# An attention and FFN kernel on one core: one segment's transposes moved from TensorE to DMA, the last output tile in column halves, and a new order of the instructions

## The chip, the core and the metric

The kernel runs on one core of a Trainium2 chip. A core has five engines that work in parallel, each through its own instructions in order: TensorE (PE, matrix products), VectorE (DVE), ScalarE (ACT), GpSimd (POOL) and SyncE (SP, which here only issues DMAs). The metric is the time of one execution on the device in microseconds (us); lower is better.

## The reference

Two identical layers work on x of 2048 tokens by 512 features in bf16. Each layer is an attention with a compressive memory (32 heads of 16, four segments of 512 tokens) and then a gated FFN of width 1376, each on a layer-normalised input and added back to x:

```python
def _A_ref(x, wq, wk, wv, wo, beta):        # x: layer-normalised
    q, k, v = ...                           # x @ wq, x @ wk, x @ wv, by heads and segments
    for s in range(4):
        p = softmax(qs @ ks.T * scale + causal_mask)
        a_dot = p @ vs
        pq = phi(qs)                        # phi(t) = t + 1 if t > 0 else exp(t)
        a_mem = (pq @ M) / (pq @ z + 1e-6)
        o = g * a_mem + (1 - g) * a_dot     # g = sigmoid(beta), one a head
        M = M + phi(ks).T @ vs
        z = z + phi(ks).sum(over tokens)
    return concat(o) @ wo

def _B_ref(x, w1, w3, w2):                  # x: layer-normalised
    return (silu(x @ w1) * (x @ w3)) @ w2

for layer in range(2):
    x = x + _A_ref(_layernorm(x), ...)
    x = x + _B_ref(_layernorm(x), ...)
```

## The kernel before

The kernel's x stays in on-chip memory as 16 tiles of 128 tokens (`x_tok`); a segment is four tiles. Both layers run through the four segments, so there are eight steps, g = 0 to 7 (g = 4 * layer + segment). Every step does the following.

- **Layer norm** (`layer_norm`): statistics of each tile on DVE (`bnst` L604, `bnag` L606), variance plus epsilon (`lnve` L609), the power -1/2 on POOL (`lnrs` L611), and the normalised tile `xn` (`norm`, L618; two tiles share an xn buffer). The products need x with the features on the partitions, so each tile is then transposed. With `turn` set, TensorE does that in four 128x128 transposes a tile into PSUM (`xt`, L628), and an engine copies the result out (`evt`). Otherwise one DMA transpose on SP's queue turns two tiles at once (`xT`, L634). Before the change `turn` holds for the attention's layer norm of g = 0 and g = 1; all other layer norms go by DMA.
- **Projections** (`project`): q and k by groups of heads (L677), v by tiles (L672), each four products that add up in a PSUM bank, then a copy out on ACT or DVE.
- **Attention** (`attention`): units of logits, four row groups of TensorE side by side (L852), one exponential on ACT for each (L861), the causal mask of the diagonal blocks on POOL (L874), and the weighted values (`attend`, L903). Their results go by a DMA transpose on SP (`XT`, L913) to the division on DVE and POOL (`normalise`, L928 to L941) and by another one (`oT`, L944) to the output projection (L952).
- **Memory** (`phi`, `memory_update`, `memory_read`): phi of k is transposed by DMA (`pkT`, L725) and contracted with v on TensorE (`dacc`, L738); phi of q reads the memory.
- **FFN** (`ffn`): gate and up products (L983), tanh on ACT (L994), two DVE operations (L996, L1000), down products (L1011), and the sum into `x_tok` (`resB`, L1016). In the last layer each tile is then stored (`stx`, issued on SP at L470).

The order on every engine comes from a list scheduler (`Sched.schedule`) that runs when the kernel is built. Each operation has an estimated duration and latency, a priority, and gates (operations that must have been placed before it). The tables `SLACK`, `LOOK`, `MARGIN`, `PRIO`, `GATE` and the constant `C_AGE` steer its choices: `PRIO` shifts the priority of the operations of one name in one step, `GATE` moves the attention unit behind which they may come, `MARGIN` makes an operation's inputs count as later, and `C_AGE` is how long a weighted-values product waits for a moment at which TensorE is not in the midst of full-size products. `dmaT` gives the scheduler its estimate for a DMA transpose. Once chosen, the order is fixed: each engine executes its list in order and waits on semaphores where an input is not ready.

The weights of the FFN and the later x tiles are loaded while step 0 runs (on SP and POOL queues). TensorE's work of later steps fills the gaps between the units of attention of earlier ones: the projections of step 1 run between the logits of step 0, the FFN of step 0 between those of step 1, and so on. After the last attention unit (in the second half of step 7) only the FFN is left.

Of the kernel before, what the change touches and what calls it, by code (L numbers as in the profile page):

```python
# [4 lines left out]
ALU = mybir.AluOpType  # L5
# [3 lines left out]
P = 128  # L9
T = 2048  # L10
# [19 lines left out]
PE_SWITCH = 100.0  # L30
PE_TAIL = 170.0
R_SLACK = 0.0
SLACK = {"pe": 30.0, "act": 60.0, "dve": 60.0, "pool": 0.0, "sp": 30.0}
LOOK = {"pe": 90.0, "act": 10.0, "dve": 10.0, "pool": 5.0, "sp": 200.0}
C_AGE = 1200.0
MARGIN = {"XT": 800.0, "bnst": 50.0, "dacc": 300.0, "evv": 200.0, "g": 100.0, "km": 2000.0, "macc": 100.0, "mde": 1200.0, "mnum": 500.0, "mrec": 200.0, "norm": 50.0, "o": 50.0, "oT": 2000.0, "rd": 200.0, "rdg": 100.0, "resB": 500.0, "stx": 3000.0, "v": 100.0, "xT": 2000.0, "xt": 500.0}


class Pool:
# [328 lines left out]
def o_pe(ns):  # L368
# [4 lines left out]


PRIO = {
    ("bnag", 1): 500.3, ("bnag", 2): 4, ("bnag", 3): 500.15, ("bnag", 4): 300, ("evX", 0): 285.6, ("evk", 1): 700,
    ("evk", 6): -299.6, ("g", 3): -0.05, ("g", 6): -5, ("gp", 0): 19.85, ("hm", 3): 1050, ("hm", 5): -50.05,
    ("k", 3): -0.6, ("k", 4): -2, ("k", 5): 21.4, ("k", 7): 0.15, ("lnve", 5): 500, ("mblk", 2): 300,
    ("mnum", 6): -950.6, ("oT", 3): -600, ("ph", 7): -20, ("phmin", 1): 0.3, ("q", 1): -300, ("q", 6): -1248.55,
    ("q", 7): 0.05, ("rd", 5): -800, ("rdg", 1): 300, ("rdg", 7): -1000, ("resA", 4): -300, ("t", 3): -1000,  # L380
    ("t", 7): -900.4, ("u", 4): -1000, ("v", 1): 2, ("v", 6): -50,
}
GATE = {
    ("bnst", 2): -4, ("bnst", 3): 2, ("bnst", 4): -1, ("km", 7): 14, ("ph", 0): -21, ("phexp", 0): -10, ("v", 0): 2,
    ("v", 1): -45, ("v", 5): -13, ("v", 6): 6, ("v", 7): 8,
}


def build(nc, A_x, A_wq, A_wk, A_wv, A_wo, A_beta, B_w1, B_w3, B_w2, out):
# [6 lines left out]
    def new(name):  # L396
        return Buf(pools[name])
# [67 lines left out]
    def pe(fn, ns, mode="F", **k):  # L465
        return S.add([o_pe(ns)], fn, mode=mode, **k)
# [2 lines left out]
        occ = 60.0 if q != "pool" else 1000.0  # L469
        return S.add([(q, occ, 2000.0)], lambda e: e.dma_start(out_ap, in_ap), dmaq=q, size=size, prio=prio, **k)  # L470

    def dmaT(fn, q="sp", **k):
        return S.add([(q, 1290.0, 2500.0) if k.pop("narrow", False) else (q, 1400.0, 3000.0)], fn, dmaq=q, mode="T", **k)

    def ev(dst, src, n, **k):

# [119 lines left out]
    def layer_norm(s, name, prio, gates=(), fine=False, turn=False, part=(0, LT), dst=None):  # L596
# [17 lines left out]
        for i in tiles:  # L614
# [7 lines left out]
            if turn:  # L622
                B = new("B")
                tb = lambda B=B: bank(B).bitcast(BF16)[:, 0:512].rearrange("p (g c) -> p g c", g=NCG)

                def flip(e, xn=xn, k=k, tb=tb):
                    for cg in range(NCG):
                        o = e.transpose(tb()[:, cg, :], xn_r[xn.slot][:, k, 128 * cg:128 * cg + 128], ident[:])  # L628
                    return o
                pe(flip, 4 * 62, reads=[(xn, k), "ident"], writes=[(B, 0)], bufs=[B, xn], prio=-900, name="xt")  # L630
                ev(lambda i=i: dt_[dst.slot][:, i, :].rearrange("p (g c) -> p g c", c=P), tb, 512, reads=[(B, 0)], writes=[(dst, i)],
                   bufs=[B, dst], prio=-900, name="evt")
            elif k == 1:
                dmaT(lambda e, i=i, xn=xn: e.dma_start_transpose(  # L634
                    dt_[dst.slot][:, i - 1:i + 1, :].rearrange("p i (g c) -> p (i g) c", c=P), xn_r[xn.slot][:].rearrange("p i d -> p (i d)")),
                     reads=[(xn, 0), (xn, 1)], writes=[(dst, i - 1), (dst, i)], bufs=[xn, dst], prio=prio, name="xT")
        return dst


# [82 lines left out]
    def memory_update(g, z, pkb):  # L722
        kt = new("W")
        for hf in range(2):
            dmaT(lambda e, hf=hf: e.dma_start_transpose(  # L725
                pkt_r[kt.slot][:, 2 * hf:2 * hf + 2, :, :].rearrange("p g i c -> p (g i) c"),
                pk_r[pkb.slot][:, 2 * hf:2 * hf + 2, :].rearrange("p g n -> p (g n)")),
                 reads=[(pkb, hf)], writes=[(kt, hf)], bufs=[pkb, kt], prio=g + 0.1, name="pkT")
        mb = new("mb")
        for hf in range(2):  # L730
            B = new("B")
# [155 lines left out]
    def attend(s, g, z, pr, part, G, ees, where, xg, gates):  # L887
# [22 lines left out]
        for a, X in enumerate(Xs):  # L910
            ev(lambda a=a: xs_r[xs.slot][:, a, :], lambda X=X: bank(X), 512, reads=[(X, 0)], writes=[(xs, a)], bufs=[X, xs],
               prio=g - 100.2, name="evX")
        dmaT(lambda e: e.dma_start_transpose(xg_r[xg.slot][:, 0:n, :], xs_r[xs.slot][:].rearrange("p a n -> p (a n)")[:, 0:128 * n]),  # L913
             reads=[(xs, a) for a in range(len(Xs))], writes=[(xg, 0)], bufs=[xs, xg], prio=pr, name="XT", narrow=n == 4)

    def normalise(g, z, part, G, xg, oms):

# [22 lines left out]
        if oms is not None:  # L940
# [2 lines left out]
                writes=[(og, 0), (og, 1)], bufs=[og, oms[G]], prio=pr, name="oadd")  # L943
        dmaT(lambda e: e.dma_start_transpose(  # L944
            ot_r[z.ot.slot][:, G, 128 * t0:128 * t1].rearrange("p (t c) -> p t c", t=nt), fl(og_r, og)),
             reads=[(og, 0), (og, 1)], writes=[(z.ot, G, t) for t in range(t0, t1)], bufs=[og, z.ot], prio=pr, name="oT", narrow=True)

    def out_proj(s, g, z, part):
        for i in range(*part):
# [10 lines left out]
    def ffn(s, g, X, part, last=False):  # L960
# [43 lines left out]
        for i in range(t0, t1):  # L1004
            B = new("B")
            tt = 4 * s + i
            for ft in range(NFT):
                fw = width(ft)
                h, c = of[ft]
# [8 lines left out]
            if last:  # L1018
                ov = out[0].rearrange("(t p) d -> p t d", p=P)
                dma("sp", ov[:, tt, :], x_tok[:, tt, :], 131072, prio=base, reads=[("x", tt)], name="stx")  # L1020


    for layer in range(2):
        for s in range(NS):
# [1 line left out]
            S.cur = g  # L1026
            n0 = len(S.ops)
            X = layer_norm(s, "xa", g - 1.0, gates=[(0, 2) if g == 1 else (0, 13) if g == 2 else (g - 2, 13)],
                           fine=(g == 0), turn=g <= 1)
            if g == 0:  # L1030
                done = [op for op in S.ops[n0:] if op.name == "bnst"][-1:]
                second_loads(LOADS + ("" if LATE_AT is not None else LATE), dict(gates=done, after=done))
# [66 lines left out]
```

The softmax here doesn't subtract the row's maximum and nothing guards it: scores larger than these inputs give would overflow.

## Time and profile before

| | |
|---|---|
| median of 6 runs | 496.1 us (493.36 to 502.42) |
| the profiled execution | 493.74 us |
| its span, first to last instruction | 492.0 us |
| mean granted TensorE clock in it | 0.995 |
| PE busy | 477.1 us, 97% |
| DVE busy | 401.2 us, 82% |
| ACT busy | 390.7 us, 79% |
| POOL busy | 251.6 us, 51% |

Durations in the text come from the profiled execution. A row of the timeline gives start and length in us, the engine, the line of the kernel, the operation, what it writes and reads, and how many instructions were merged; the bracket at its end gives the idle time of the engine before it and what ended that. In the table by stage each engine's busy time in the stage stands with its number of instructions, then the granted clock, the share of the DMA engines and the GB/s they moved. In the list of waits, the total, the number and the longest wait follow the pair that waited and was waited for. Matmuls overlap, so the length of one matmul holds both its streaming time and its latency: the distance of the starts in a row of equal ones is what it costs.

### The profile page before, as it was taken

Reading aid. Unit: us, or ns where it says so; the run is one execution under the profiler, and the core shown is the slowest. Engines: PE = TensorE matmul, PEld = TensorE weight load, DVE = VectorE, ACT = ScalarE, POOL = GpSimd, SP = SyncE. Lnnn points to the kernel's source line nnn. Section 1 sums busy time; section 2 is a strip of 40 time slices with the busy share of each in tenths; the row PEclk is TensorE's granted clock in tenths of the full one; section 3 lists DMA queues with packets and bytes.
Section 4 is the critical chain, followed back from the end, with each engine's and each line's share of the span. In section 5 each row is a group of like instructions: output and inputs, shape, how many; then the busy total and the mean of one; then the engine's idle time right before and its main releaser. Section 6 shows DMA issues by size and latency. Waiting matters only on the chain.

```text
span 492.0 us, 10341 instructions
## 1 busy us (share of the span) xinstructions
PE 477.1 (97%) x4155; PEld 216.6 (44%) x4198; DVE 401.2 (82%) x803; ACT 390.7 (79%) x344; POOL 251.6 (51%) x379
## 2 busy tenths in 40 slices
PE   8989999999999999999999999899999999999997
PEld 4434346754444444334443444444444434444443
DVE  5899999997998888889976899688984687478672
ACT  3979998988988987899888999689987989830230
POOL 4847555765565546556554447565564546520000
PEclk9989999999999999999999999999999999999999
DMA  8665843331233334432442515521153215210301
GB/s 281 222 103 129 150 81 71 77 68 41 55 75 71 64 54 57 61 65 55 66 87 23 86 24 103 69 55 34 32 87 75 46 23 76 76 32 15 82 1 43
DMA packets 101983, 35.84 MB, mean 73 GB/s; under 512 B 94800, under 2 KB 99920, under 8 KB 101936
## 3 DMA queue, kind: packets, MB, share of 16 engines
q1 hardware_dynamic: 99488, 30.36, 30.2%
q0 software_dynamic: 1488, 4.03, 4.1%
q10 hardware_dynamic: 960, 0.79, 0.5%
q8 instruction: 33, 0.54, 0.5%
q14 instruction: 14, 0.11, 0.1%
HBM read 8.43 MB, written 2.10 MB: 21 GB/s over the span
## 4 chain that ended last, share of the span: by engine, by line
PE 79%; DVE 10%; ACT 8%; DMA 2%; issue 1%; POOL 0%; DVEq 0%
PE psall L983 29%; PE psall L1011 15%; PE psall L852 9%; PE psall L677 8%; PE psall L903 6%; ACT e L861 6%; PE psall L952 4%; PE psall L672 4%; DMA W<-W 1%; DVE ln L604 1%; ACT px L712 1%; DVE W L480 1%; DVE xn L618 1%; PE psall L738 1%; DVE x_tok L956 1%
## 5 line engine op out<-in xcount | busy, mean ns | idle before, releaser
L861 ACT ACTIVATE e<-psall 128x2048 bf16<-128x2048 f32 (+1 forms) x180 | 301.5, 1710 | 39.6 <-PE psall L852 37.4
L874 POOL TENSOR_SCALAR_AFFINE_SELECT e<-e 128x512 bf16<-128x512 bf16 x256 | 164.2, 661 | 157.9 <-ACT e L861 157.2
L983 PE MATMUL psall<-W,w 128*128 128x512 bf16 (+2 forms) x792 | 172.6, 357 | 0.4 <-DVE gp L996 0.2
L983 PEld LDWEIGHTS psall<-W,w 128*128 128x128 bf16 (+1 forms) x792 | 73.7, 100 | 74.5 <-issue 12.4
L1011 PE MATMUL psall<-w,h 128*128 128x512 bf16 (+1 forms) x332 | 82.1, 380 | 1.4 <-issue 0.8
L994 ACT ACTIVATE th<-psall 128x512 bf16<-128x512 f32 (+1 forms) x89 | 51.1, 593 | 35.0 <-PE psall L983 34.9
L996 DVE SCALAR_TENSOR_TENSOR gp<-th,psall 128x512 bf16<-128x512 bf16 (+1 forms) x89 | 58.7, 673 | 19.6 <-ACT th L994 18.9
L1000 DVE SCALAR_TENSOR_TENSOR h<-gp,psall 128x512 bf16<-128x512 bf16 (+1 forms) x89 | 59.7, 672 | 8.7 <-PE psall L983 8.1
L1011 PEld LDWEIGHTS psall<-w,h 128*128 128x128 bf16 (+1 forms) x352 | 32.5, 98 | 38.2 <-issue 5.6
L604 DVE BATCH_NORM_STATS2 ln<-x_tok 128x6 f32<-128x512 bf16 x64 | 42.8, 684 | 1.2 <-DMA x_tok<-in_A_x_dram 0.6
L852 PE MATMUL psall<-W 16*128 16x256 bf16 (+3 forms) x544 | 41.8, 295 | 1.4 <-ACT e L861 0.8
L1016 DVE TENSOR_TENSOR x_tok<-psall,x_tok 128x512 bf16<-128x512 f32 x32 | 22.0, 688 | 25.8 <-PE psall L1011 25.7
L852 PE MATMUL psall<-W,km 32*128 32x256 bf16 (+3 forms) x544 | 41.3, 292 | 0.6 <-ACT e L861 0.6
L903 PE MATMUL psall<-e,va 128*32 128x256 bf16 (+3 forms) x1088 | 41.2, 293 | 0.6 <-DVE x_tok L1016 0.2
L480 DVE CAST W<-psall 128x512 bf16<-128x512 f32 x51 | 34.1, 680 | 5.0 <-PE psall L677 4.8
L936 POOL TENSOR_TENSOR og<-xg,rd 128x256 bf16<-128x256 bf16 (+1 forms) x40 | 26.9, 679 | 20.6 <-DVE rd L930 16.4
L677 PE MATMUL psall<-W,wk 128*128 128x512 bf16 (+1 forms) x144 | 35.4, 357 | 0.9 <-ACT W L479 0.9
L480 DVE CAST xs<-psall 128x512 bf16<-128x512 f32 x40 | 26.8, 683 | 10.2 <-PE psall L903 10.1
L618 DVE TENSOR_SCALAR xn<-x_tok,ln 128x512 bf16<-128x512 bf16 x64 | 32.8, 546 | 2.8 <-POOL ln L611 2.8
L672 PE MATMUL psall<-wv,W 128*128 128x512 bf16 x116 | 32.8, 391 | 1.0 <-issue 0.3
L677 PE MATMUL psall<-W,wq 128*128 128x512 bf16 (+1 forms) x144 | 33.1, 357 | 0.3 <-issue 0.3
L852 PEld LDWEIGHTS psall<-W 16*128 16x128 bf16 x544 | 13.2, 91 | 44.6 <-ACT e L861 38.5
(65 smaller groups left out, 447.6 us busy)
## 6 DMA issues: line engine op xcount, KB each, us to landing
w<-in_B_w_dram SPq DMA_DIRECT2D x4, 688.0 KB, 8.2
out_dram<-x_tok SPq DMA_DIRECT2D x16, 128.0 KB, 1.7
km<-W POOLq DMA_DIRECT2D x24, 64.0 KB, 2.9
w<-in_B_w_dram POOLq DMA_DIRECT2D x3, 384.0 KB, 3.9
x_tok<-in_A_x_dram POOLq DMA_DIRECT2D x2, 512.0 KB, 5.0
xg<-xs SPq DMA_TRANSPOSE x36, 2.8
W<-og SPq DMA_TRANSPOSE x36, 2.4
wk<-in_A_wk_dram SPq DMA_DIRECT2D x1, 512.0 KB, 4.2
```

What stands on the lines that cost most here:

```text
L480: return e.tensor_copy(dst(), src())
L672: fn = lambda e, cg=cg, G=G, B=B, st=st, sp_=sp_: e.matmul(bank(B), xa_r[X.slot][:, G, 128 * cg:128 * cg + 128], wv_sb[:, cg, :], start=st ...
L677: fn = lambda e, cg=cg, G=G, B=B, st=st, sp_=sp_, w=w, a=a, W=W, c0=c0: e.matmul(bank(B)[:, W * a:W * a + W], w[:, cg, 128 * G:128 * G + 1 ...
L852: o = e.matmul(S4[:, sps(pg), c:c + n], kk[32 * pg:32 * pg + r, G, 128 * j:128 * j + 128], q_r[z.q.slot][32 * pg:32 * pg + r, G, 128 * t1 ...
L861: act(lambda e, N=N, ebuf=ebuf, pgs=pgs, sps=sps: e.activation(e_r[ebuf.slot][:, pgs[0]:pgs[-1] + 1, 0:N], S4[:, sps(pgs[0]):sps(pgs[-1]) ...
L874: pool(lambda e, ebuf=ebuf, c=c: e.affine_select(e_r[ebuf.slot][:, :, c:c + 128], e_r[ebuf.slot][:, :, c:c + 128], pattern=[[0, 4], [1, 128]],
L903: o = e.matmul(bank(X)[32 * pg:32 * pg + 32, base + W - n:base + W], va_r[z.va.slot][:, j, h:h + 32], e_r[eb.slot][:, pg, c:c + n], start= ...
L983: prev = pe(lambda e, i=i, cg=cg, ft=ft, B=B, w=w: e.matmul(bank(B)[0:width(ft), W * i:W * i + W], w[:, cg, 128 * ft:128 * ft + width(ft)] ...
L994: act(lambda e, fw=fw, NW=NW, B=B, th=th: e.activation(th_r[th.slot][0:fw, 0:NW], bank(B)[0:fw, 0:NW], ACT.Tanh, scale=0.5), NW, reads=[(B ...
L996: dve(lambda e, fw=fw, NW=NW, B=B, th=th, gp=gp: e.scalar_tensor_tensor(gp_r[gp.slot][0:fw, 0:NW], th_r[th.slot][0:fw, 0:NW], 1.0, bank(B) ...
L1000: dve(lambda e, fw=fw, NW=NW, B=B, gp=gps[fg], h=hs[fg]: e.scalar_tensor_tensor(h_r[h.slot][0:fw, 0:NW], gp_r[gp.slot][0:fw, 0:NW], 0.5, b ...
L1011: prev = pe(lambda e, ft=ft, fw=fw, B=B, h=h, c=c: e.matmul(bank(B), h_r[h.slot][0:fw, c:c + 128], w2_sb[0:fw, ft, :], start=(ft == 0), st ...
```

## The change

Four edits. (1) The attention's layer norm of step g = 1 goes by two DMA transposes of two tiles each in place of sixteen TensorE transposes and four copies. (2) The very last output tile is computed in two halves of 256 columns, each with its own sum and its own store. (3) The scheduler's estimate of a DMA transpose's occupancy is 1250 ns for all, and its latency is given by kind. (4) The steering tables have new values, so the order of the instructions on every engine is a new one.

```diff
-SLACK = {"pe": 30.0, "act": 60.0, "dve": 60.0, "pool": 0.0, "sp": 30.0}
-LOOK = {"pe": 90.0, "act": 10.0, "dve": 10.0, "pool": 5.0, "sp": 200.0}
-C_AGE = 1200.0
-MARGIN = {"XT": 800.0, "bnst": 50.0, ...}
+SLACK = {"pe": 30.0, "act": 30.0, "dve": 60.0, "pool": 60.0, "sp": 60.0}
+LOOK = {"pe": 90.0, "act": 60.0, "dve": 5.0, "pool": 60.0, "sp": 10.0}
+C_AGE = 4000.0
+MARGIN = {"bnag": 500.0, "bnst": 300.0, ...}
...
 PRIO = {
...
+    ("bnag", 3): 0.05, ("bnag", 4): 301, ("bnag", 7): 0.3, ("bnst", 1): -500, ("bnst", 5): 500.15, ("d", 3): -500,
...
 GATE = {
-    ("bnst", 2): -4, ("bnst", 3): 2, ("bnst", 4): -1, ("km", 7): 14, ("ph", 0): -21, ("phexp", 0): -10, ("v", 0): 2,
-    ("v", 1): -45, ("v", 5): -13, ("v", 6): 6, ("v", 7): 8,
+    ("bnst", 2): -17, ("bnst", 3): 1, ("ph", 0): -22, ("phexp", 0): -6, ("v", 0): 2, ("v", 1): -59, ("v", 3): 2,
+    ("v", 7): 8,
 }
...
-    def dmaT(fn, q="sp", **k):
-        return S.add([(q, 1290.0, 2500.0) if k.pop("narrow", False) else (q, 1400.0, 3000.0)], fn, dmaq=q, mode="T", **k)
+    def dmaT(fn, lat, q="sp", **k):
+        return S.add([(q, 1250.0, lat)], fn, dmaq=q, mode="T", **k)
...
+            if last and i == LT - 1 and ENDS > 1:
+                n = finish(s, g, tt, t0, of, base, step, n, prev)
+                continue
...
+    ENDS = 2
+
+    def finish(s, g, tt, t0, of, base, step, n, prev):
+
+        ov = out[0].rearrange("(t p) d -> p t d", p=P)
+        for c0 in range(0, D, D // ENDS):
+            cs, B = slice(c0, c0 + D // ENDS), new("B")
+            for ft in range(NFT):
...
+                prev = pe(lambda e, ft=ft, fw=fw, B=B, h=h, c=c, cs=cs: e.matmul(
+                    bank(B)[:, 0:D // ENDS], h_r[h.slot][0:fw, c:c + 128], w2_sb[0:fw, ft, cs], start=(ft == 0), stop=(ft == NFT - 1)),
...
+            dve(lambda e, B=B, cs=cs: e.tensor_tensor(x_tok[:, tt, cs], bank(B)[:, 0:D // ENDS], x_tok[:, tt, cs], ALU.add), D // ENDS, True,
...
+            dma("sp", ov[:, tt, cs], x_tok[:, tt, cs], 131072 // ENDS, prio=base, reads=[("x", tt, c0)], name="stx")
...
-                           fine=(g == 0), turn=g <= 1)
+                           fine=(g == 0), turn=g <= 0)
```

The latencies given by kind are 3300 ns for xT and pkT (3000 before), 2400 for oT and the narrow XT (2500 before) and 2800 for the wide XT (3000 before).

## The prediction

> **What bounds the kernel now.** I read the page's engine table first, then the waits of TensorE, then tables by stage, and then the timeline of the one stage that stood out.
>
> ```profile
> PE 477.1 (97%) x4155; PEld 216.6 (44%) x4198; DVE 401.2 (82%) x803; ACT 390.7 (79%) x344; POOL 251.6 (51%) x379
> PEclk9989999999999999999999999999999999999999
> ```
>
> TensorE (PE) is busy nearly all the time and no other engine is near it. So a microsecond in which PE stands still, or does work it need not do, is a microsecond of the total: after segment 0 there is always projection or FFN work queued on it. The second row has one lower digit, the third slice (24.6 to 36.9 us). The table by stage, 24 to 42 us in steps of 6, and the waits of PE and of ScalarE (ACT) there:
>
> ```profile
> core 0: us, PE busy (x) PEld busy (x) DVE busy (x) ACT busy (x) POOL busy (x), PEclk, DMA share, GB/s
> 24.00:30.00 6.00, 4.55 (x68) 2.04 (x68) 5.42 (x8) 6.00 (x7) 5.01 (x8) 0.99 1.15 146
> 30.00:36.00 6.00, 5.84 (x40) 2.16 (x37) 5.11 (x13) 3.51 (x4) 0.48 (x1) 0.72 0.38 77
> 36.00:42.00 6.00, 6.00 (x92) 3.10 (x89) 5.62 (x18) 6.00 (x9) 2.89 (x6) 1.00 0.25 68
> ...
> PE psall L628 <- DVE xn L618: 1.3, 1, 1.3
> ...
> ACT e L861 <- PE psall L852: 2.5, 2, 2.2
> ```
>
> PE idles, then runs at a granted clock of 0.72, and ACT, full before and after, has 2.5 us without logits. The timeline names the cause:
>
> ```profile
> 26.27 2.89 DVE L618 TENSOR_SCALAR xn<-x_tok,ln 128x512 bf16<-128x512 bf16 x1
> ...
> 27.67 0.27 PE L852 MATMUL psall<-W,km 32*128 32x256 bf16 x2
> 29.22 0.40 PE L628 MATMUL psall<-ident,xn 128*128 128x128 bf16 x4 [1.28 <-DVE xn L618]
> ...
> 31.02 0.63 PE L628 MATMUL psall<-ident,xn 128*128 128x128 bf16 x4
> ```
>
> L628 is segment 1's TensorE transpose. It stands in PE's in-order stream behind a normalisation (L618) that took 2.89 us where its neighbours take 0.40; everything behind it, the logits for ACT included, waits. So the path around 27 to 34 us is this transpose, not ACT.
>
> **The change, part by part.** All against the profiled execution, 493.74 us with a span of 492.0; the median of the runs shown is 496.1, 2.4 more, and I carry the difference over.
>
> *Transposes off PE.* The 1.28 us wait at 29.22 goes, because no PE instruction reads xn of segment 1 any more. The slow clock cost (1 - 0.99) x 6 + (1 - 0.72) x 6 = 1.74 us. Sixteen transposes go: a group of four lasts 0.40 and one alone 0.219, so they start (0.40 - 0.219) / 3 = 0.06 apart and cost 16 x 0.06 = 0.97. Some ran in the slow stretch and are counted twice there, 0.2 off. Sum: 1.28 + 1.74 + 0.97 - 0.2 = 3.8 us. The four 0.40 us copies of their results leave VectorE (DVE), 1.6 us of a 93% busy stretch; that only speeds the casts that PE waits for now and then, and I book nothing for it.
>
> [...]
>
> *Transposes onto the DMA queue.* Two more issues on SP, 1.3 us each there. The same shape (W<-xn, 28 of them) lands 3.0 to 5.7 us after issue:
>
> ```profile
> L634 SPq DMA_TRANSPOSE W<-xn x28: 1231/1306/3075, 52.9 to 456.7; - x28
> ...
> DMA to landing us min/median/max: 3.0/3.2/5.7
> ```
>
> In today's order the last normalisation ends at 31.02 + 0.39 = 31.4, so x would land at 34.6 to 37.1; today the last copy ends at about 38.0 (37.58 + 0.42). So x is not later, but it comes in two lumps, and PE has less to fill with in between: today segment 1's V products run between 32 and 38. Without filler PE has 0.32 us of logits per exponential of 5.61 / 6 = 0.94, thus 0.62 idle of each 0.94. Four microseconds of that would be 2.6, less two memory contractions of 0.55. Bounds 0 to 2.6; the new order raises segment 1's statistics (bnst, 500 earlier; they start at 16.2 now though their load went out at 5.96), so I take the low side, +0.7. On SP the two issues wait for L618, and behind them in line stand XT and pkT, which go out between 24 and 33 us; those feed the division of segment 0's outputs and the memory contraction. SP issues nothing from 33.4 to 40.96, so a wait of some microseconds there is taken up again, and I book none.
>
> [...]
>
> *The last tile by halves.* The end of the timeline:
>
> ```profile
> 488.76 0.69 DVE L1016 TENSOR_TENSOR x_tok<-psall,x_tok 128x512 bf16<-128x512 f32 x1 [1.69 <-PE psall L1011]
> 489.48 0.33 SPq L470 DMA_DIRECT2D out_dram<-x_tok  x1
> ```
>
> 22 matmuls of 256 columns (L677 at 8.66 us: 8 last 1.05, one 0.27, so 0.11 apart) replace 11 of 512 (43 in 9.46: 0.216 apart): 2.44 against 2.37, +0.07. The last add is half as wide: 0.41 for a 256-column DVE operation from PSUM in this profile (L996's 96x256 form), against 0.69, -0.28. Then a 64 KB store in place of 128 KB (1.7 us to landing): between 0 and -0.3, I take -0.1, as the fixed part of 1.7 us should dominate. Nothing hides this, it is the end of the chain. Sum -0.3; bounds -0.5 and +0.1.
>
> *The new order and latencies.* All other queues may be reordered. From 60 to 480 us PE's listed waits that are real (a DMA, ACT, DVE) come to 1.0 for the contraction at L738, 0.6 for ACT and about 1.2 in pieces of 0.2: at most -2.8 to gain. To lose there is more: one late transpose costs about what L738's wait did, 1.0, and a new order may hold several; I bound it at +4. Value 0, as neither sign has a row for it.
>
> Sum: -3.8 + 0.7 - 0.3 + 0 = -3.4: 490.3 for a profiled execution, 492.7 beside the median of 496.1. Own range: stall term from 0 to 2.6, so -4.1 to -1.5, 492.0 to 494.6.
>
> **The rivals.** *The wait only moves (same).* The normalisation at 26.27 is what was late; if it stays late and slow (GpSimd's masks run at 25.44 to 29.0 beside it), PE will wait at segment 1's first projection instead. For it: DVE is over 90% busy there. Against: PE can go on with logits meanwhile, so ACT stays fed. Only the transposes and the end are won: -0.97 - 0.3 = -1.3, 494.8.
>
> *Segment 1's x comes too late (slower).* SP issues in order. If an xT is placed behind the XT that goes out at 40.96, it lands at about 42.2 + 3.2, the second at 46 to 47. PE has run out of filler at about 33.5; each later microsecond costs 0.62 / 0.94 = 0.66. Break-even is where this eats 3.8 + 0.3 = 4.1 us, x at 39.7; slower by 2.5 us takes 6.6 / 0.66 = 10 us, x at 43.5. With x at 45, the first landing, the idle time is 7.6, +3.5: 499.6. For it: early landings are the slow ones (median 4.0 us for the XT before 60 us, 2.8 over the run), since the weights share the DMA engines. Against: SP is idle in between, and nothing forces that place.
>
> *More is won.* The order also closes the other waits: -3.4 - 2.8 = -6.2, 489.9. For it are only the 2.8 us themselves.
>
> That the change does not do what it says has little room: the 16 transposes are gone from PE by a flag.
>
> **How the numbers follow.** Forecast 0.46, wait moves 0.22, x too late 0.22, more won 0.10. About 0.5% (2.5 us) is what a measurement of this kernel can tell from no change. The last third of the forecast's range lies within it; as its likely values crowd at the other end I give that 0.06. Faster: 0.40 + 0.10 = 0.50; same: 0.22 + 0.06 = 0.28; slower: 0.22. The range runs from 489.5 (-6.6, just past the best case) to 500.0 (+3.9, half of the late case beyond it): 0.11 + 0.04 are left out. It holds cases of both signs; the likeliest one's range is 492.0 to 494.6.
>
> **What would show it.** Right: 16 records of the transpose line in place of 32, no PE wait for xn behind 20 us, granted clock 1.00 from 30 to 36 us, ACT's 2.2 us wait gone, 30 W<-xn transposes with two before 40 us landing in 3 to 6 us, 17 output stores, the last add near 0.41 us. Wrong: the slow clock is still there or has moved; PE waits at segment 1's projections for a DMA; new PE waits over 1 us behind 60 us, which would make the order, not the transposes, the main term.

## The result and the profile after

The change made the kernel slower. The ratio of its time to the time before, on the same chip, is 1.0065, with a 95% interval of 1.0049 to 1.0081. The median is 498.52 us (495.29 to 502.41, 32 runs) beside 494.74 us for the kernel before (67 runs, which take the place of the six of the table). So 0.0065 x 494.74 = 3.2 us were lost, where a gain of 3.4 was forecast (the two medians lie 3.8 us apart; the ratio, from runs on the same chip, is the better measure). The profiled execution of the changed kernel took 497.77 us, with a span of 496.0 and a mean granted clock of 0.990 (before 0.995).

The page's engine table and its row of the TensorE clock, after:

```profile
PE 478.5 (96%) x4185; PEld 220.0 (44%) x4226; DVE 394.7 (80%) x796; ACT 393.6 (79%) x350; POOL 250.3 (50%) x380
PEclk9987999999999999999999999999999999999999
```

PE executes 4185 matmuls in place of 4155 (16 transposes fewer, 44 products more from the halves of four tiles; a trace can miss a few records) and is as busy as before. The clock row has two low digits where there was one. The table by stage of the changed kernel, 24 to 48 us:

```profile
core 0: us, PE busy (x) PEld busy (x) DVE busy (x) ACT busy (x) POOL busy (x), PEclk, DMA share, GB/s
24.00:30.00 6.00, 5.62 (x76) 2.28 (x76) 5.31 (x8) 6.00 (x8) 5.43 (x9) 1.00 1.03 159
30.00:36.00 6.00, 3.13 (x25) 1.33 (x26) 6.00 (x17) 3.83 (x5) 0.46 (x1) 0.70 1.08 171
36.00:42.00 6.00, 6.00 (x57) 2.45 (x56) 2.82 (x12) 4.13 (x6) 2.63 (x4) 0.50 0.15 36
42.00:48.00 6.00, 6.00 (x81) 2.40 (x80) 5.35 (x14) 5.50 (x7) 4.70 (x8) 0.95 0.53 136
```

This is the main reading. Between 30 and 36 us PE is busy for 3.13 of 6 us, in 25 matmuls (before: 5.84, in 40). Between 36 and 42 it is busy all the time, but at half clock: 57 matmuls in place of 92. ACT, full there before, has 4.13. The clock costs (0.30 + 0.50 + 0.05) x 6 = 5.1 us of PE time, where the stages from 24 to 36 us cost 1.74 before. The slow stretch has not gone; it is three times as dear.

What PE waited for between 20 and 100 us (total, number, longest), and its timeline from 29 us:

```profile
PE psall L737 <- DVE va L479: 1.9, 1, 1.9
PE psall L851 <- ACT e L860: 1.5, 2, 0.8
PE psall L902 <- POOL e L873: 0.9, 1, 0.9
PE psall L982 <- DVE om L781: 0.6, 1, 0.6
```

```profile
29.18 0.60 PE L671 MATMUL psall<-wv,W 128*128 128x512 bf16 x2
30.50 0.28 PE L851 MATMUL psall<-W 16*128 16x256 bf16 x2 [0.71 <-ACT e L860]
30.62 0.27 PE L851 MATMUL psall<-W,km 32*128 32x256 bf16 x2
32.78 1.09 PE L737 MATMUL psall<-va,W 128*128 128x136 bf16 x8 [1.89 <-DVE va L479]
33.80 0.40 PE L851 MATMUL psall<-W 16*128 16x256 bf16 x4
...
34.76 0.63 PE L671 MATMUL psall<-wv,W 128*128 128x512 bf16 x1 [0.33 <-issue]
```

After the last V products of segment 0 at 29.2 us PE has four small logits products (16 and 32 rows) and then waits 1.89 us for a copy of V (`va`) before the first memory contraction. Segment 1's first full product starts only at 34.76 (two products of that form last 0.60 us at 29.18 and, at half clock, 1.03 at 36.07). The same time on DVE, on GpSimd (POOL) and on SP's queue:

```profile
26.88 2.72 DVE L617 TENSOR_SCALAR xn<-x_tok,ln 128x512 bf16<-128x512 bf16 x1
...
29.78 0.72 DVE L617 TENSOR_SCALAR xn<-x_tok,ln 128x512 bf16<-128x512 bf16 x2
...
32.10 0.62 DVE L479 CAST va<-psall 128x512 bf16<-128x512 f32 x1
```

```profile
25.89 3.56 POOL L873 TENSOR_SCALAR_AFFINE_SELECT e<-e 128x512 bf16<-128x512 bf16 x6
```

```profile
30.21 2.61 SPq L633 DMA_TRANSPOSE W<-xn  x2
```

The first normalisation of segment 1 is again late and long (2.72 us, as 2.89 before) beside six of GpSimd's masks, and holds up the copies of V behind it on DVE. The two transposes go out from 30.21 on and land 3.3 and 3.1 us after their issue, so x comes in two lumps, at 33.5 and 34.7 us.

Where the time is lost can be followed on one milestone per step. The first exponential of step 1 starts at 59.27 us after, 56.85 before: 2.42 later, of which 0.44 are there from the start. The last exponential of the kernel starts at 432.40, before at 428.62: 3.78 later. So some 2 of the 3.3 us that arise between start and last exponential arise before 60 us. The other part shows from 60 to 120 us (before, then after, same columns as in the table by stage):

```profile
60.00:120.00 60.00, 58.78 (x625) 33.63 (x621) 55.34 (x116) 54.48 (x46) 35.09 (x54) 1.00 0.35 71
```

```profile
60.00:120.00 60.00, 56.72 (x627) 32.41 (x631) 53.78 (x111) 53.47 (x46) 35.17 (x55) 1.00 0.44 71
```

PE is busy for 2.06 us less at full clock, in new waits at 61, 67 and 87 us.

The end, the two last sums on DVE:

```profile
491.51 0.42 DVE L1040 TENSOR_TENSOR x_tok<-psall,x_tok 128x256 bf16<-128x256 f32 x1 [0.51 <-PE psall L1035]
492.71 0.42 DVE L1040 TENSOR_TENSOR x_tok<-psall,x_tok 128x256 bf16<-128x256 f32 x1 [0.78 <-PE psall L1035]
```

From the start of the last product to the landing of the last store it is 2.30 us, before 2.83: 0.53 won. But SP then goes through its closing semaphore waits one by one, most of them 0.06 us after the one before (in the trace of after one takes 0.37), and the span ends 1.32 us behind that landing, before 0.83. From last product to end the two kernels differ by 0.04 us (3.62 and 3.66).

**One number for a run.** A profile is one execution; the granted clock and the span are known for every one. Clock lost = (1 - mean granted clock) x span. The kernel before has a slow state, which 15 of its executions in the experiments show, with 12 to 16 us lost, and which this comparison leaves out. Before, the median over the other 91 runs is 1.5 us (10th to 90th percentile 0 to 3.5); after, it is 8.4 over 32 runs (3.6 to 11.9). A line through the runs gives a span of 491.2 + 0.94 x lost before and 491.6 + 0.62 x lost after (correlations 0.83 and 0.94). At no lost clock the two kernels would be within 0.4 us of each other. The profiled execution of after, with 5.0 lost, is one of its milder ones. The traces list the clock itself: it is 1.00 or 0.50 and nothing between. Before, it is 0.50 for 3.41 us from 29.9 us on; after, for 10.24 us from 32.4 on (each trace has one more such stretch, which begins at about the program's end). Clock lost goes through the experiments; it adds up all slow stretches of a run, wherever they lie.

### The profile page after: what moved, and what is told of

Read it like the earlier page. It is cut to its first block, busy times and chain, and to the rows that moved or that the text cites. A ratio compares the mean times of both kernels' runs of the same rounds, so it can differ in the third digit from the quotient of the medians.

```text
span 496.0 us, 10405 instructions
## 1 busy us (share of the span) xinstructions
PE 478.5 (96%) x4185; PEld 220.0 (44%) x4226; DVE 394.7 (80%) x796; ACT 393.6 (79%) x350; POOL 250.3 (50%) x380
## 4 chain that ended last, share of the span: by engine, by line
PE 76%; DVE 11%; ACT 7%; DMA 3%; issue 2%; POOL 0%; ACTq 0%; DVEq 0%
PE psall L982 28%; PE psall L1013 14%; PE psall L851 9%; PE psall L676 8%; PE psall L902 7%; ACT e L860 5%; PE psall L951 4%; PE psall L671 3%; PE psall L1035 2%; DMA xg<-xs 2%; DVE xn L617 1%; DVE W L715 1%; PE psall L737 1%; DVE va L479 1%; DVE gp L995 1%
## 5 line engine op out<-in xcount | busy, mean ns | idle before, releaser
L982 PE MATMUL psall<-W,w 128*128 128x512 bf16 (+3 forms) x792 | 171.1, 356 | 1.3 <-DVE om L781 0.6
L993 ACT ACTIVATE th<-psall 128x512 bf16<-128x512 f32 (+2 forms) x89 | 51.4, 594 | 35.9 <-PE psall L982 35.3
L995 DVE SCALAR_TENSOR_TENSOR gp<-th,psall 128x512 bf16<-128x512 bf16 (+2 forms) x89 | 58.9, 672 | 19.3 <-ACT th L993 18.7
L1013 PE MATMUL psall<-w,h 128*128 128x512 bf16 (+1 forms) x291 | 71.6, 380 | 1.3 <-issue 0.5
L1013 PEld LDWEIGHTS psall<-w,h 128*128 128x128 bf16 (+1 forms) x308 | 28.2, 98 | 34.7 <-issue 5.2
L479 DVE CAST W<-psall 128x512 bf16<-128x512 f32 x46 | 31.1, 681 | 8.2 <-PE psall L676 7.8
L1018 DVE TENSOR_TENSOR x_tok<-psall,x_tok 128x512 bf16<-128x512 f32 x28 | 19.3, 688 | 21.2 <-PE psall L1013 21.2
L676 PE MATMUL psall<-W,wq 128*128 128x512 bf16 (+1 forms) x144 | 35.2, 360 | 0.0
L902 PEld LDWEIGHTS psall<-e,va 128*32 128x32 bf16 x1088 | 24.3, 97 | 20.1 <-issue 3.2
```

Source lines behind the costliest of these rows:

```text
L479: return e.tensor_copy(dst(), src())
L676: fn = lambda e, cg=cg, G=G, B=B, st=st, sp_=sp_, w=w, a=a, W=W, c0=c0: e.matmul(bank(B)[:, W * a:W * a + W], w[:, cg, 128 * G:128 * G + 1 ...
L902: o = e.matmul(bank(X)[32 * pg:32 * pg + 32, base + W - n:base + W], va_r[z.va.slot][:, j, h:h + 32], e_r[eb.slot][:, pg, c:c + n], start= ...
L982: prev = pe(lambda e, i=i, cg=cg, ft=ft, B=B, w=w: e.matmul(bank(B)[0:width(ft), W * i:W * i + W], w[:, cg, 128 * ft:128 * ft + width(ft)] ...
L993: act(lambda e, fw=fw, NW=NW, B=B, th=th: e.activation(th_r[th.slot][0:fw, 0:NW], bank(B)[0:fw, 0:NW], ACT.Tanh, scale=0.5), NW, reads=[(B ...
L995: dve(lambda e, fw=fw, NW=NW, B=B, th=th, gp=gp: e.scalar_tensor_tensor(gp_r[gp.slot][0:fw, 0:NW], th_r[th.slot][0:fw, 0:NW], 1.0, bank(B) ...
```

## The experiments

Theory A: PE has too little to do between 30 and 34 us because segment 1's x comes in two lumps by DMA, its clock falls to half and stays there, and that is the loss. Rivals: the 1.89 us wait for `va` is the root and any order without it is fast; the half clock is only a sign and the new order loses the time elsewhere; the tail or the DMA queues lose it.

All edits but one (interleaved normalisation) leave the scheduler alone. They change its finished order: `move(a, b)` puts operation a behind b on its engine, `fill(n, b, d)` puts n idle 512-column products on TensorE behind b, into the PSUM bank that d is to use and before d, and `find` picks an operation by engine, name and step. All else keeps its place. Ratios are to the kernel before on the same chip; medians taken on different chips are compared less closely than ratios.

**The wait for `va` taken away.** The memory contraction goes behind segment 1's last V product.

```diff
 # the changed kernel
+self.move(self.find("pe", "dacc", 0), self.find("pe", "v0.3", 1))
```

> The changed kernel with one instruction group moved: segment 0's first memory contraction goes behind segment 1's first four V products on TensorE. Theory A (the loss is made early: TensorE stands 2.05 us in front of this contraction at 30.6 us, and the half clock of 10.2 us follows from that idle stretch): the wait for the cast of va goes, ACT's 2.2 us wait for logits at 34.4 shrinks, the slow clock falls to one window of 3.4 us or none, total 2 to 5 us below the changed kernel, ratio to the kernel before 0.997 to 1.002. Rival B (the loss comes from the new order behind 60 us): the total stays within 1 us of the changed kernel, ratio 1.005 or more.

Measured: 496.43 us, 1.0066 [1.0043, 1.0089], as after. Clock lost 5.7. PE's waits between 20 and 100 us:

```profile
PE psall L904 <- ACT e L913: 2.5, 4, 0.8
...
PE psall L724 <- DMA W<-xn: 0.9, 1, 0.9
```

The wait for `va` is gone, and four waits for ACT and one for x itself stand in its place. The ratio is the rival's (1.005 or more), but not for the rival's reason: the slow stretch is still there, 6.83 us from 33.6 us on. So the wait for `va` was not the root: PE had nothing to do, whatever it waited for.

**Idle products as filler.** Three before the small logits at 30.5 us and eight before the contraction, all of full size (128 rows).

```diff
 # the changed kernel; d = self.find("pe", "dacc", 0)
+self.fill(3, self.find("pe", "v3.3", 0), d)
+self.fill(8, self.find("pe", "R1.3", 0), d)
```

> The changed kernel with 11 idle 512-column products added on TensorE, 3 in front of the logits at 30.5 us and 8 in front of the contraction that waits; nothing else is moved and their results are overwritten. Theory A with the clock as the carrier: the waits stay, but the granted clock stays at 1.00 between 30 and 43 us, and the total falls by about half of the slow 10.2 us, 3 to 5 us, ratio 0.997 to 1.001. Rival (the slow clock is not owed to the idle stretch, or the waits alone make the loss): granted clock as in the changed kernel, the total the same or up to 2.4 us longer, ratio 1.005 to 1.012.

Measured: 495.23 us, 1.0024 [1.0006, 1.0043], clock lost 1.5. By stage, 30 to 42 us:

```profile
30.00:36.00 6.00, 5.30 (x41) 1.88 (x41) 6.00 (x16) 4.44 (x6) 0.98 (x2) 1.00 0.80 154
36.00:42.00 6.00, 6.00 (x85) 2.68 (x86) 5.49 (x20) 6.00 (x8) 4.60 (x7) 1.00 0.35 91
```

Eleven products whose results nobody reads make the kernel 0.4% faster. The clock is 1.00, PE does 85 matmuls from 36 to 42 in place of 57 (none of them idle ones, which end at 32.8), and ACT is full again. But PE, now earlier, waits 2.7 us, from 55.7 to 58.4 us, for a transpose of the attention's output (`oT`, W<-og), and the one slow stretch that is left in this trace, 3.41 us, begins at 58.3. That wait is the second loss.

**The tail alone.** The halves put into the kernel before (the function `finish` and its call, nothing else).

```diff
 # the kernel before
+if last and i == LT - 1 and ENDS > 1:
+    n = finish(s, g, tt, t0, of, base, step, n, prev)
+    continue
```

> The kernel before with the column halves alone (the flag holds for the last tile of each of the last layer's four segments). Theory: the last store lands 0.5 us sooner behind the last product, but SP's closing waits run one after another and give it back, so the span behind the last product stays at 3.6 us and the total within 0.5 us of the kernel before, ratio 0.998 to 1.002. Rival (my prediction): 0.3 us won.

Measured: 494.74 us, 1.0013 [0.9988, 1.0038]. An interval of 0.25%, 1.2 us, on either side can't tell 0.3 us from none. The profile can: from the start of the last product to the end it is 3.41 us, in place of 3.66 before: 2.32 to the landing of the last store, and 1.09 behind it. So 0.25 us were won, near the 0.3 forecast, and the expectation that all of it is given back did not hold in this kernel; in the changed kernel it does (3.62).

This run shows something else. Around 30 us PE does there what it does in the kernel before, in the same order and with the same wait for `xn`, but the slow stretch is not there:

```profile
PE psall L628 <- DVE xn L618: 1.3, 1, 1.3
```

```profile
30.00:36.00 6.00, 5.88 (x52) 2.29 (x49) 6.00 (x15) 4.80 (x7) 1.23 (x2) 1.00 0.38 76
```

So a wait of 1.3 us there can lower the clock and need not.

**The transposes alone.** Segment 1's x goes by DMA; every other instruction stands in the place it had in the kernel before.

```diff
 # the kernel before, its finished order kept as a list
-                           fine=(g == 0), turn=g <= 1)
+                           fine=(g == 0), turn=g <= 0)
```

> The kernel before with segment 1's transposes by DMA and every other instruction in its old place on every engine. Theory A: TensorE's next filler, segment 1's first V product, now stands in line until the first DMA transpose has landed, at 33 to 34 us; TensorE idles 3 us there, the clock halves, and the total is 1 to 5 us above the kernel before, ratio 1.002 to 1.010. Rival (my prediction): the stall at the transposes is gone, 1 to 3 us won, ratio 0.993 to 0.998; then the new order alone makes the loss.

Measured: 500.66 us, 1.0126 [1.0093, 1.0159], clock lost 10.0. PE's timeline and the table by stage from 30 to 54 us:

```profile
33.54 1.03 PE L738 MATMUL psall<-wv,W 128*128 128x512 bf16 x2 [3.79 <-DMA W<-xn]
```

```profile
30.00:36.00 6.00, 2.46 (x8) 0.39 (x8) 2.89 (x8) 2.17 (x3) 0.00 (x0) 0.69 0.77 146
36.00:42.00 6.00, 6.00 (x41) 1.97 (x44) 3.92 (x8) 4.39 (x6) 1.23 (x2) 0.50 0.00 0
42.00:48.00 6.00, 6.00 (x61) 2.69 (x53) 2.85 (x12) 4.03 (x6) 2.49 (x4) 0.50 0.34 89
48.00:54.00 6.00, 6.00 (x55) 2.00 (x53) 3.07 (x10) 4.55 (x5) 4.05 (x6) 0.50 0.52 110
```

The new transposes by themselves cost 1.26%, above Theory A's range; the new order takes about half of that back (ratios 1.0126 and 1.0065). One wait of 3.79 us brings 23.89 us of half clock, from 32.2 to 56.1 us, in which PE is 100% busy by the stages from 36 us on.

**Filler in the kernel before.** Five idle products before segment 1's first TensorE transpose.

```diff
 # the kernel before
+self.fill(5, self.find("pe", "R1.2", 0), self.find("pe", "xt", 1))
```

> The kernel before with five idle 512-column products on TensorE (1.1 us) in front of the first transpose of segment 1, which waits 1.3 us there; nothing else is moved. Theory C (what separates executions and kernels is time at half clock, which an idle stretch of a microsecond or more around 30 us sets off): the slow window of some executions goes, the clock lost (one minus the mean granted clock, times the span) falls from a median of 1.5 us to under 0.7, the median falls by 0.5 to 1.5 us, ratio 0.996 to 1.000. Rival (the slow windows come at random, whatever TensorE does): clock lost and time as before, ratio 0.999 to 1.003.

Measured: 492.86 us, 0.9975 [0.9945, 1.0005], clock lost 0.0. The point is in line with the 1.5 us that the kernel before loses by its clock; the interval just holds 1.

**The loads away from the output transposes.** Three loads of w2 and one of x leave POOL's queue between 44 and 55 us and go out after 76.

```diff
 # the changed kernel; masks: GpSimd's masks of step 1 behind km of step 2
+loads = [self.find("pool", "ldw2", 0, i) for i in (2, 3, 4)] + [self.find("pool", "ldx", 0, 1)]
+for n, op in enumerate(loads):
+    self.move(op, masks[n])
```

> The changed kernel with four loads on GpSimd's queue (three of w2, one of x, 1.1 MB) moved from 44 to 55 us to behind 76 us; they are needed from 86 us on. Theory D (between 48 and 62 us these loads slow the DMA transposes, and TensorE waits for what hangs on them): the 1.0 us wait in front of the weighted values at 61 us and the one for phi(k)'s transpose at 67 us go, the landing of the transposes between 48 and 62 us falls below 4 us, 1 to 2 us below the changed kernel, ratio 1.001 to 1.005. Rival (the order, not the loads, makes these waits): within 0.7 us of the changed kernel.

Measured: 498.82 us, 1.0105 [1.0067, 1.0142], neither theory's number. The transposes `oT` did get faster. From issue to landing (median us, 44 to 64 us), first after, then this kernel:

```profile
W<-og SPq DMA_TRANSPOSE x6, 3.5
```

```profile
W<-og SPq DMA_TRANSPOSE x6, 2.4
```

PE's waits at 61 and 67 us are gone, but the slow clock stays from 34.4 to 51.4 us (17.07 us); the runs lose 8.9 us at the median. While PE is late for the clock, the loads are not what it is late for.

**Both mended in the changed kernel, and both in the kernel before.**

```diff
 # the changed kernel: the fill(3), fill(8) and the loads moved, as above
 # the kernel before: the fill(5) and the loads moved, as above
```

> The changed kernel with both the 11 idle products of the second experiment and the late loads. Theories C and D together: the clock stays at 1.00 behind 30 us, and TensorE's 2.7 us wait for the outputs' transpose at 55 us, which appeared when the idle products alone were added, falls under 1 us; 1.5 to 3 us below that experiment, ratio 0.994 to 0.999, under the kernel before. Rival (the wait at 55 us is only the next of a series and moves on): ratio 1.001 to 1.004.

> The kernel before with the five idle products and the same four loads late. If theories C and D hold for it as well, the waits at 55 us (0.8) shrink and the clock stays up: ratio 0.993 to 0.998, and against the one above it shows what the change itself is worth once both losses are gone: by my prediction's remaining terms (transposes 1.0, end 0.3) the changed kernel should then be 1 us faster. Rival: no gain beyond that of the idle products.

Measured: the changed kernel 492.26 us, 0.9973 [0.9951, 0.9995]; the kernel before 492.33 us, 0.9970 [0.9945, 0.9996]; clock lost 0.0 in both. This is the test of the whole account: with clock and loads mended no difference between the two kernels is left that these runs could show (0.07 us between the medians). Each ratio is known to about 0.25%, 1.2 us, so the 1 us that was expected for the changed kernel is not excluded. The second loss of the changed kernel shows only where the first is mended. Filler first takes 0.41% (1.0065 to 1.0024), the loads then 0.51%. The loads first take nothing, filler then 1.3% (1.0105 to 0.9973). In the kernel before, filler takes 0.25% and the loads 0.05%, both within the intervals.

**Normalisation with interleaved access.** The four normalisations read and write with an interleave of 256 elements; the author's guess was that GpSimd's masks would then not hold them up.

```diff
 # the changed kernel, L617, slow for step 1 alone
+slow = lambda t: t.rearrange("p (a b) -> p b a", a=2)
-e.tensor_scalar(xn_r[xn.slot][:, k, :], x_tok[:, tt, :], ...
+e.tensor_scalar(slow(xn_r[xn.slot][:, k, :]), slow(x_tok[:, tt, :]), ...
```

> The changed kernel with segment 1's four normalisations on VectorE reading and writing the same elements in another order (the two halves of a row interleaved, so that neighbours in the access are 256 elements apart); every order is kept. [...]

Measured: 500.06 us, 1.0112 [1.0068, 1.0157], clock lost 7.2. The first normalisation took 3.88 us and the others 1.4 to 1.6, so the edit made DVE slower and did not free it:

```profile
PE psall L738 <- DVE va L479: 5.6, 1, 5.6
```

So it says nothing on the cause of the slow normalisation. It trebles PE's wait, 5.6 us in place of 1.9, and the point lies 0.5% higher; the interval overlaps that of the changed kernel, so a higher cost is not shown.

**Filler that is busy but small.** The eleven idle products use 16 rows of the array.

```diff
 # the changed kernel with its filler
-e.matmul(..., wq_sb[:, 0, 0:128], wq_sb[:, 0, :], ...)
+e.matmul(..., wq_sb[0:16, 0, 0:128], wq_sb[0:16, 0, :], ...)
```

> The second experiment again, its 11 idle products with 16 rows of the array in place of 128; duration and place are the same. If the clock follows the time in which TensorE executes anything, the result is that of the second experiment: clock lost about 1.3 us, ratio 1.000 to 1.004. If it follows how much of the array works (which would also say why the slow stretch outlasts the wait, as it is full of logits of 16 and 32 rows), the clock falls as without them: clock lost 4 us or more, ratio 1.006 to 1.012.

Measured: 498.01 us, 1.0058 [1.0032, 1.0085], clock lost 5.0.

```profile
30.00:36.00 6.00, 5.53 (x35) 2.19 (x36) 6.00 (x17) 3.83 (x6) 0.80 (x2) 0.67 0.98 155
36.00:42.00 6.00, 6.00 (x58) 2.45 (x58) 2.82 (x13) 4.12 (x6) 2.54 (x4) 0.50 0.23 60
```

PE is as busy as with the full filler (5.53 and 5.30 from 30 to 36 us) and the clock falls all the same: 0.67 and 0.50 with 16 rows, 1.00 and 1.00 with 128. So in these two runs it was not PE's busy time that held the clock; what differed is the rows of the array that the idle products use. That the wait is filled does not help either: the time is that of the changed kernel without filler.

**The masks as the cause of the slow normalisation.** The six masks beside it cover 2 columns in place of whole blocks.

```diff
 # the changed kernel, six masks behind lnrs of step 1
-e.affine_select(e_r[slot][:, :, c:c + 128], ...)
+e.affine_select(e_r[slot][:, :, c:c + 2], ...)
```

> The changed kernel with the six GpSimd masks that overlap segment 1's first normalisation (25.9 to 29.4 us) cut from 128 to 2 columns a head group, so part of the causal mask of segment 0 is left out; every order is kept. If GpSimd's masks hold VectorE up, the first normalisation falls from 2.7 to about 0.4 us, the cast of va ends about 2 us sooner, TensorE's 1.9 us wait falls under 0.5, clock lost to a median of 4 us or less: ratio 0.998 to 1.003. If they don't, the normalisation stays over 2 us, ratio 1.005 or more.

Measured: 498.92 us, 1.0081 [1.0049, 1.0114], clock lost 10.4. DVE's timeline, PE's waits and the next stages:

```profile
29.12 0.33 DVE L678 TENSOR_SCALAR xn<-x_tok,ln 128x512 bf16<-128x512 bf16 x1
```

```profile
PE psall L798 <- DMA W<-W: 0.9, 1, 0.9
```

```profile
30.00:36.00 6.00, 4.42 (x35) 1.66 (x35) 4.23 (x12) 4.87 (x6) 0.10 (x1) 0.83 1.26 155
36.00:42.00 6.00, 5.86 (x52) 1.80 (x52) 3.86 (x10) 4.67 (x6) 2.74 (x4) 0.50 0.24 46
```

The masks are what stretches the normalisation: 0.33 us in place of 2.72. The long wait for `va` goes with it, but the half clock stays (20.48 us from 33.9 on), as x still comes when its DMA lands. Cause of the slow normalisation and cause of the loss are two things. The profiled execution is not a clean test of the second: a slow stretch of 3.41 us at 10 us makes it late from the start, and its two transposes land 5.1 and 3.1 us after issue, at 35.4 and 36.3 us, later than in the changed kernel. The runs' median of 10.4 us lost stands without it.

The normalisation of the changed kernel, from 26.88 to 29.60 us, ends with the last of the six full masks (29.45). How the masks hold DVE up no run here shows.

**x earlier.** The statistics' power goes ahead of a load on POOL, the four normalisations five places forward on DVE, the transposes one place forward on SP; then the same with loads and closing waits mended (below), and with filler too.

```diff
 # the changed kernel
+o.remove(lnrs); o.insert(o.index(ldx), lnrs)
+at = self.find("dve", "phmin", 0, 0)
+for n in range(4):
+    op = self.find("dve", "norm", 1, n)
+    self.move(op, at); at = op
+self.move(sp[i - 1], xts[1])     # the XT ahead of the two xT goes behind them
```

> The changed kernel with segment 1's power on GpSimd in front of the load issue, its four normalisations on VectorE five places earlier and its two transposes on SP one place earlier; TensorE's order is kept and nothing is added. Segment 1's x lands at 29 to 31 us in place of 33.5, the cast of va is no longer behind a slow normalisation, and the wait of 1.9 us goes: clock lost median 2 to 5 us, ratio 0.998 to 1.004. Rival (the six places only move the same stall onto the casts of q and of the weighted values, and TensorE waits there): ratio 1.005 or more.

> The kernel of the last experiment with the late loads and the ordered closing waits, no idle products: 1 to 2.5 us below it if the clock stays up, ratio 0.993 to 0.999; if the clock still falls in the stretch without filler work around 30 us, 1.000 to 1.004.

> The same with the 11 idle products as well. If idle products and early normalisations mend the same loss, it equals the better of the two, ratio 0.993 to 0.996; if early normalisations shorten the wait itself, the idle products now stand in TensorE's way by up to 2 us, 0.996 to 1.000.

Measured: 499.85 us, 1.0112 [1.0075, 1.0150], clock lost 10.5; with loads and closing 498.43 us, 1.0059 [1.0017, 1.0101], 10.4; with filler 494.13 us, 1.0004 [0.9980, 1.0029], 1.5. In the first of them:

```profile
24.63 5.20 DVE L688 TENSOR_SCALAR xn<-x_tok,ln 128x512 bf16<-128x512 bf16 x4
```

The normalisations start 2.25 us earlier and now stand beside the masks, all four: 5.20 us. PE waits 1.3 us for a copy queued behind them. Nor did x come at 29 to 31 us, as expected: the two transposes went out at 27.0 and 29.9 but landed 5.4 and 3.4 us later, at 32.4 and 33.3, only 1.0 and 1.4 us sooner than in the changed kernel. So an x that is really early was not tested. DVE's order gave to the one what it took from the other.

**The best of both.** Filler, loads and an order of SP's closing waits by when each semaphore's last operation ends.

```diff
 # the changed kernel; and the kernel before with its own fill(5), the loads and the halves
-for lane, v in sorted(finals.items()):
+for lane, v in sorted(finals.items(), key=lambda x: ends[x[0]]):
```

> The changed kernel with the 11 idle products, the late loads, and SP's closing waits in the order in which the queues end (the last store's queue is waited for last). The closing waits behind the last landing fall from 1.3 us to about 0.5: 0.5 to 0.8 us below the seventh experiment, ratio 0.994 to 0.998. Rival: the closing waits overlap the landing already, ratio 0.997 as there.

> The kernel before with the five idle products, the late loads, the column halves and the ordered closing waits. With the last landing 0.5 us sooner and the closing waits 0.3 us shorter, 0.5 to 0.9 us below the eighth experiment: ratio 0.993 to 0.997. Rival: within 0.3 us of it.

Measured: the changed kernel 491.04 us, 0.9945 [0.9918, 0.9972]; the kernel before 492.29 us, 0.9957 [0.9929, 0.9985]. The changed one by stage:

```profile
30.00:36.00 6.00, 5.88 (x49) 2.05 (x48) 6.00 (x11) 5.71 (x7) 2.88 (x5) 1.00 1.31 144
36.00:42.00 6.00, 5.38 (x76) 2.42 (x76) 5.49 (x16) 4.75 (x7) 2.63 (x4) 1.00 0.48 93
```

The span ends 0.49 us behind the last landing in place of 1.32 (0.47 in the kernel before, mended), and from the start of the last product to the end it is 2.78 us in both, in place of 3.60 and 3.66. Both profiled executions lose clock in another place, at the start: 6.83 us at 0.50 from 8.7 us on, and 3.41 us from 10.1 on in the kernel before. No experiment here bears on that place. With the new closing waits the changed kernel is faster than both kernels given; the intervals of the two mended ones overlap, so which of them is the better is not settled.

## Why the prediction was wrong

**The step that failed** is the term "transposes onto the DMA queue", +0.7 with bounds 0 to 2.6. It saw rightly that PE would lack filler once x comes in lumps, and took 0.62 us of idle time in each 0.94 from rows at full clock. Then it priced the gap by its idle time alone. The gap's real price is what it does to the clock: 5.1 us in the profile, 8.4 at the median of the runs, for waits of 0.7 and 1.9 us amid sparse products. For the transposes alone the prediction has -3.8 + 0.7 = -3.1 us; in the old order they cost 1.26%, +6.2 us. The prediction's own rows had the case in them: a wait of 1.28 us stood there beside 1.74 us of lost clock.

**The slow clock booked as a gain.** The -1.74 us supposed that the slow stretch hung on the wait for `xn`, and that the wait's end would end it. It hung on the lack of large products on PE: with eleven idle ones of 128 rows the clock is 1.00 from 30 to 42 us, where the changed kernel has 0.70 and 0.50. The wait did end, the lack grew, and so did the slow stretch. Nor does the wait always bring it, as the run with the halves alone shows. The term's size was also that of one execution; that the median over 91 runs is 1.5 was luck.

**The rival that held** is "segment 1's x comes too late": slower because PE runs out of filler at about 33.5 us or sooner. Its mechanism is right, its place and threshold are not. It needed the two transposes behind the XT at 40.96 us and x at 43.5; they went out at 30.21, x came at 33.5 and that was enough, because its price of 0.66 us for each us left out the clock, and because filler ended at 29.8 in the new order. The time, 498.52, lies in the range given, and on the side with a chance of 0.22.

**The order** was booked at 0, bounds -2.8 to +4. It takes back about half of what the transposes cost in the old order (0.61%, some 3 us, with the tail's part in it), and it brings output transposes together with loads: 0.51% once the clock is held, 2.5 us, where the kernel before shows 0.05%. Both signs are there, the gain at its bound and the loss inside. The second was not foreseen: the prediction priced reordered transposes by PE's waits in the trace of before, and not by what is loaded beside them (3.5 us to landing beside the loads, 2.4 with the loads moved).

**The tail** was to bring -0.3. To the landing it brought 0.53; the waits that SP has left there gave 0.49 of it back (1.32 - 0.83). In the kernel before the same halves won 0.25 us to the end. So the term was nearly right by itself; what it left out is what follows the store, the order of SP's closing waits, which is another one in the changed kernel. The widths were right: the sums took 0.42 us (0.41 forecast), and a store of 64 KB landed 1.5 us after its issue, one of 128 KB 1.7. The count was not: `last` holds for the whole last layer, so it is not the very last tile alone that is halved but the last tile of each of its four segments, with 20 stores in place of the 17 expected.

**Right** were: 16 transposes left on PE and none waited for in segment 1, two DMA transposes landing in 3.3 and 3.1 us (within 3 to 6), issued before 40 us; and the time to landing of a transpose, taken from the rows (3.0 to 5.7 us). "The slow clock is still there" was named as what would show the forecast wrong, and it is what is seen.

**Left open:** what starts a slow stretch in one execution and not in another, and what ends it (10.24 us in the trace of after, 23.89 with the transposes alone); why moving the loads alone brought no gain at all (1.0105, 8.9 us of clock lost); whether a really early x would do what filler does; and how the order's two effects divide, as its parts were not tried one by one.

## What to carry to other kernels

Price a gap on TensorE at its clock as well as at its length (here waits of 0.7 and 1.9 us went with 5.1 us of lost clock), and before dense work is taken off TensorE, name what will fill its place: here the removed transposes, and the V products they let through tile by tile, were the filler. Compare executions by clock lost as well as by time, since one profile is one draw (5.0 us lost in the profile of after, a median of 8.4 over its runs). A few idle full-size products are a cheap test, and here were a remedy (1.0065 to 1.0024). Loads that can wait were better kept away from the transposes here, though only once the clock was held (1.0024 to 0.9973).

## What the runs showed of the hardware

- **Busy is not dense.** With the transposes alone PE was busy for 6.00 of 6.00 us in three stages on end (36 to 54 us) at a clock of 0.50. Idle products of 128 rows kept the clock at 1.00 from 30 to 42 us; the same with 16 rows did not (0.67, then 0.50). From 36 to 42 us the changed kernel shows 6.00 us busy with 57 matmuls at 0.50, the kernel before 6.00 with 92 at 1.00, so the busy column hides the loss.
- **The clock's steps.** The slow stretches inside the programs last 3.41 us (before), 6.83 (contraction moved), 10.24 (after), 17.07 (loads moved), 20.48 (small masks) and 23.89 us (transposes alone), that is 1, 2, 3, 5, 6 and 7 times 3.41. The runs show the same step: before, most mean clocks lie near 1.000, 0.9965 and 0.993, steps of 0.0035 x 492 = 1.7 us of lost clock, which is 3.4 us at half clock. Before, a slow stretch began at 29.9 us, 0.7 us behind the end of a wait of 1.28 us; after, one began at 32.4 us, within a wait of 1.89. With the halves alone the same wait of 1.3 us stood there and the clock was 1.00 from 30 to 36 us.
- **DVE beside GpSimd's masks.** A normalisation of 128x512 took 2.72 us beside six full masks (after) and 0.33 beside cut ones; four of them beside full masks took 5.20 (normalisations early). With interleaved access it took 1.4 to 1.6 us without masks and 3.88 beside them (after, without interleave: some 0.4 and 2.72).
- **Closing waits cost.** SP's last semaphore waits come 0.06 us apart for the most part, and with another order of them the end lay 0.49 us behind the last landing in place of 1.32.
- **Loads and transposes.** Output transposes landed in 3.5 us beside loads on POOL's queue (after) and in 2.4 with the loads moved (44 to 64 us, medians of six); with filler in both, in 4.1 and 2.3 (46 to 62 us).
